# A single-core decode step: the last w_down rows in three transfers, ScalarE's softmax as a loop, one section at the end

## The chip, the cores and the metric

The kernel runs on one core of a Trainium2 chip. The metric is the device time of one execution in microseconds. The profile is one execution, taken by the hardware profiler; its span runs from the core's first instruction to its last.

In the profile PE is TensorE (matmul) and PEld its weight load, DVE is VectorE, ACT is ScalarE, POOL is GpSimd, and SP is the engine that issues nearly all loads. PEq, SPq and so on are the sequencers of these engines. DMA stands for the core's 16 DMA engines together.

## The reference, cut to what matters

One token (x has 1 x 1024 elements) passes through an attention block with a cache and a gated feed-forward block, in bf16.

```python
def _A_ref(x, k_cache, v_cache, wq, wo):        # 32 query heads, 4 key heads, 65536 keys of 128
    q = (x @ wq).reshape(B, Sq, Hq, Dh)          # k and v are repeated for the 8 heads of each group
    scores = einsum("bhqd,bhkd->bhqk", q, k) * Dh ** -0.5
    o = einsum("bhqk,bhkd->bhqd", softmax(scores), v)
    return o.reshape(B, Sq, Hq * Dh) @ wo

def _B_ref(x, w_gate, w_up, w_down):             # 1024 -> 3584 -> 1024
    return (gelu(x @ w_gate) * (x @ w_up)) @ w_down

h   = x + _A_ref(layernorm(x), k_cache, v_cache, wq, wo)
out = h + _B_ref(layernorm(h), w_gate, w_up, w_down)
```

Keys and values are 67 MB each, and the weights some 39 MB; all of it is read once.

## The kernel before

**Loads.** A ring of four slots of 4096 KB in on-chip memory (`slot`) takes every large load. SP issues them in one order: the two halves of wq, then for each step t of eight (four key heads, two halves of the keys) one load of V (8192 KB) into slots 0 and 1 and two of K (4096 KB each) into slots 2 and 3 for the next step, then wo, w_gate, w_up and w_down. SP waits on counters ahead of an issue: `s_qk` counts finished score chunks and frees K's slots, `s_step` counts five events of each step and frees V's slots. The five are the transpose of the maxima, their spread over all partitions, the first and the last of 64 matmuls that fill `acc`, and the last of four that make o (`o_ps`). What is issued is worked off in order by 16 DMA engines, each of which carries a sixteenth of every 128-partition transfer.

**A step of the loop.** VectorE transposes a chunk of K (`k_chunk`), TensorE multiplies it with the query (L450), VectorE transposes the scores back (`score`). After four chunks VectorE finds the maxima and spreads them with TensorE's help (`softmax`); ScalarE takes the exponentials in eight activations, one for each head of the group; TensorE multiplies them with V into `acc`; ScalarE copies `acc` to memory (`acc_copy`) and TensorE folds it into o. TensorE's side is a hardware loop of eight rounds (`pe_loop`); the loops of VectorE, ScalarE, GpSimd and SP are written out, instruction by instruction.

**Who orders the work.** The class `Flow` records the operations of the first part (everything up to the product of the gate and up branches) and writes them out engine by engine, with a counter of its own for each engine (`done_...`). A scheduler adds the switches between such hand-written sections and the rest: at a switch the engines wait for each other's counters.

**The end.** w_down has 28 rows for each partition. 16 come first (`wa`, the "first part"), then 8 (`wb`, the "eight rows"), then 3 and then 1 into a buffer of their own, `w_end`, by two transfers (L615) with semaphores of their own; the second is issued once VectorE is through with the first part (L610). TensorE keeps itself busy with four filler matmuls (`stay_busy`), multiplies the 16 rows as wide rows (`down_wide`, 32 matmuls), ScalarE copies the sums (L655), TensorE runs three more fillers and adds the copy to the result (`add_wide`, 8 matmuls), then multiplies the 8 rows (`down`, 64 matmuls of L624), the 3 rows (24 matmuls) and the last one (8 matmuls). The wide rows are one section, the eight rows another; the copy and the adding stand between them. VectorE and ScalarE cast the two halves of the result (L667, L668), and SP stores it.

Of the kernel before, what the change touches and what calls it, by code (L numbers as in the profile page):

```python
# [16 lines left out]
class Flow:  # L17


    def __init__(self, nc, tc):  # L20
        self.nc = nc
        self.tc = tc
        self.eng = dict(pe=nc.tensor, dve=nc.vector, act=nc.scalar, pool=nc.gpsimd, sp=nc.sync)
        self.sem = {e: tc.alloc_semaphore("done_" + e) for e in self.eng}
        self.ops = []
        self.writer = {}
        self.readers = {}
        self.rows = None, None
        self.landed = {}
# [36 lines left out]
    def loop(self, body):  # L66
        self.ops.append(dict(e="pe", call=body, loop=True, dma=False, inc=None))
# [14 lines left out]
    def issue(self):  # L82
        wanted = {j for o in self.ops for j in o.get("deps", ())}
        assert all(self.ops[j]["inc"] is None for j in wanted)
        count = dict.fromkeys(self.eng, 0)
        known = {e: {} for e in self.eng}
        token = {}
        for i, o in enumerate(self.ops):
            e = o["e"]
            if "loop" in o:  # L90
                o["call"]()
                continue
            if "given" in o:
                s, v = o["landed"]
                token[i] = (s.name, s, v, {})
                continue
            mine = known[e]
            waits = [(s.name, s, v, {}) for s, v in o["wait"]] + [token[j] for j in o["deps"]]
            for name, sem, v, seen in waits:
                if mine.get(name, 0) < v:  # L100
                    self.eng[e].wait_ge(sem, v)  # L101
                    mine[name] = v
                for n, x in seen.items():
                    mine[n] = max(mine.get(n, 0), x)
            ins = getattr(self.eng[e], o["call"])(**o["kw"])  # L105
            if o["inc"]:
                ins.then_inc(*o["inc"])
            elif o["dma"]:
                s, v = o["landed"]
                ins.then_inc(s, 16)  # L110
                token[i] = (s.name, s, v, dict(mine))
            elif i in wanted:
                count[e] += 1
                ins.then_inc(self.sem[e], 1)
                token[i] = ("done_" + e, self.sem[e], count[e], dict(mine))
# [3 lines left out]
def kernel(  # L119
# [14 lines left out]
    P = 128  # L134
# [77 lines left out]
    s_qk, s_step = [tc.alloc_semaphore("from_pe_%d" % i) for i in range(2)]  # L212
    STEPS = 5
# [9 lines left out]
    f.dma("act", x_in[:], A_x[0, 0].rearrange("(u v j) -> u v j", u=XU, j=DC), w=["x_in"], r=["ones_f"], sem=tc.alloc_semaphore("x_landed"))  # L223
# [17 lines left out]
    def v_load(t):  # L241
        g, h = divmod(t, NH)
        n0 = h * CPH * CH
        f.dma("sp", slot(0, 2).rearrange("p (n d) -> p n d", d=Dh), v_v[g][:, n0:n0 + CPH * CH, :], after=["R0", "R1"],
              wait=[(s_step, STEPS * t - 1)] if t else [], inc=(s_v, 16))
# [26 lines left out]
    op("pool", "tensor_copy", r=["ident_f"], w=["ident_bf"], out=ident_bf[:], in_=ident_f[:])  # L272
# [13 lines left out]
    select("o_of", o_of[:], ALU.is_ge, 0.0, 15, [[16, 8]], -1)  # L286
    HR = 30
# [44 lines left out]
    def rows_to_columns(banks, bkeys, key, order="p n -> p n", **sizes):  # L332

        w = [ps.shape[-1] for ps in banks]
        r = over(28672, [sum(w)])
        o = 0
        for ps, n, bk in zip(banks, w, bkeys):
            src = ps.rearrange(order, **sizes)
            op("dve", "transpose", r=[bk], w=[key], out=r[:, o:o + n].rearrange("p (e j) -> p e j", j=32) if sizes else r[:, o:o + n], in_=src)
            o += n  # L340
        return r[:, 0:o:32]
# [8 lines left out]
    op("dve", "tensor_copy", r=["q_r"], w=["q_bf"], out=q_bf[:].rearrange("p b m -> p (b m)"), in_=rows_to_columns(q_banks, ["B6", "B7"], "q_r"))  # L350
# [22 lines left out]
    op("pool", "memset", w=["qs"], ap=qs[:], constant=0.0)  # L373

# [14 lines left out]
    def score(t, c):  # L389
        n = t * CPH + c  # L390
        op("dve", "transpose", w=["sc%d" % c], wait=[(s_qk, n + 1)] + ([(s_step, STEPS * t - 2)] if t and c == 0 else []),
           out=sc[:, c].rearrange("p n h s -> p (n h s)"), in_=bank[n % 2][:])
        if c == CPH - 1:
            op("dve", "tensor_reduce", r=["sc%d" % x for x in range(CPH)], inc=(from_dve, 1), out=mx1[:],
               in_=sc[:].rearrange("p c n h s -> p h (c n) s"), axis=AX.XY, op=ALU.max)

    def o_copy(t):
        g, h = divmod(t, NH)
        op("dve", "tensor_copy", w=["o_raw%d" % t], wait=[(s_step, STEPS * t + 5)], out=o_raw[:, g, h, :], in_=o_ps)

    def softmax(t):
# [4 lines left out]
        op("dve", "tensor_scalar", w=["nb%d" % t], wait=[(s_step, STEPS * t + 2)], out=nb[:, g, h, :], in0=bc_ps, scalar1=-scale, scalar2=None, op0=ALU.mult)  # L406
        for r in range(rep):
            last = r == rep - 1
            op("act", "activation", r=["nb%d" % t] if r == 0 else [], w=[] if last else ["lp%d_%d" % (t, r)],
               inc=(from_act, 1) if last else None,  # L410
               out=pt[:].rearrange("p c n h s -> p (c n) h s")[:, :, r, :], in_=sc[:].rearrange("p c n h s -> p (c n) h s")[:, :, r, :],
               func=ACT.Exp, bias=nb[:, g, h, r:r + 1], scale=scale, accum_out=lp[:, g, h, r:r + 1])

    def acc_copy(t):
        op("act", "copy", wait=[(s_step, STEPS * t + 4)], inc=(from_act, 1), out=acc_sb[:], in_=acc[:])

    for t in range(NT2):
# [14 lines left out]
        if t + 1 < NT2:  # L432
            acc_copy(t)
# [4 lines left out]
    def pe_loop():  # L438
        v_sb = slot(0, 2).rearrange("p (c s n d) -> p c s n d", c=CPH, s=NS, d=Dh)
        with nc.Fori(0, NT2, engines=(mybir.EngineType.PE,), head_slot={mybir.EngineType.PE: 0}):  # L440
# [18 lines left out]
            for c in range(CPH):  # L459
                for n in range(NN):  # L460
# [6 lines left out]
                    if (c, n) == (CPH - 1, NN - 1):  # L467
                        m.then_inc(s_step, 1)
# [12 lines left out]
    op("dve", "tensor_tensor", r=keys("nb"), w=["mn"], out=mn[:], in0=nb[:, :, 0, :], in1=nb[:, :, 1, :], op=ALU.min)  # L481
    for h in range(NH):
        op("dve", "tensor_tensor", r=["mn"], w=["df%d" % h], out=df[:, :, h, :], in0=mn[:], in1=nb[:, :, h, :], op=ALU.subtract)
    op("act", "activation", r=["df0", "df1"], w=["fa"], out=fa[:], in_=df[:], func=ACT.Exp)
# [4 lines left out]
    acc_copy(NT2 - 1)  # L489
# [5 lines left out]
    for h in range(NH):  # L495
        op("dve", "tensor_tensor", r=["rl"], w=["wt%d" % h], out=wt[:, :, h, :], in0=fa[:, :, h, :], in1=rl[:], op=ALU.mult)
    o_copy(NT2 - 1)
    ow = sb("ow", [P, Hkv, NH, rep])
    op("dve", "tensor_tensor", r=["wt0", "wt1"] + keys("o_raw"), w=["ow"], out=ow[:], in0=o_raw[:], in1=wt[:], op=ALU.mult)
# [29 lines left out]
    f.dma("sp", wv[:, HC:Hq, :], wo_v[:, HC:Hq, :], w=["R3"], wait=done, sem=r_sem[2])  # L529
    for c in range(Hq):  # L530
# [26 lines left out]
    def ffn_in(wmat, key, s0, b0):  # L557
# [4 lines left out]
        f.dma("sp", wv, wmat.rearrange("(p c) n -> p c n", p=P), w=rk, sem=r_sem[s0], wait=[(s_step, STEPS * NT2 - 1)])  # L562
# [6 lines left out]
    op("dve", "tensor_tensor", r=["g_r"], w=["t1"], out=t1[:], in0=g_sb, in1=g_sb, op=ALU.mult)  # L569
    op("dve", "tensor_scalar", r=["t1"], w=["t1"], out=t1[:], in0=t1[:], scalar1=0.044715, scalar2=1.0, op0=ALU.mult, op1=ALU.add)  # L570
    op("dve", "tensor_tensor", r=["t1", "g_r"], w=["t1"], out=t1[:], in0=t1[:], in1=g_sb, op=ALU.mult)
# [3 lines left out]
    op("dve", "tensor_scalar", r=["g_r"], w=["hg"], out=hg[:], in0=g_sb, scalar1=0.5, scalar2=None, op0=ALU.mult)  # L575
# [24 lines left out]
    op("dve", "tensor_tensor", r=["u_r", "gl", "actz"], w=["actz"], out=actz[:, :, AZ], in0=u_r, in1=gl[:], op=ALU.mult)  # L600
# [3 lines left out]
    wb_src = B_w_down[P * FA:F, :].rearrange("(p e) n -> p e n", p=P)  # L604
# [9 lines left out]
    for i, (e1, e2) in enumerate(((FB - FZ, FB - 1), (FB - 1, FB))):  # L614
        d = nc.sync.dma_start(out=w_end[:, e1 - FB + FZ:e2 - FB + FZ, :], in_=wb_src[:, e1:e2, :])  # L615
        d.then_inc(end_sem[i], 16)
        tc.no_tile_sem_insts.add(d.ins.name)
        tc.keep_in_program_order(d)
        ends.append((d, e1, e2))

    def down(a_row, w_row, landed=None):
        for j in (0, 4, 1, 5, 2, 6, 3, 7):
# [3 lines left out]
            if landed is not None:  # L626
                tc.declare_no_dep(mm.ins, landed.ins, query=mybir.DependencyQuery.ANY, reason="TensorE waits for the load's own semaphore ahead of it")
# [8 lines left out]
    def down_wide(a_row, w_row, e, n):  # L636
        for h in range(DS):
            q = 2 * (e % 2) + h
            nc.tensor.matmul(e_ps[32 * q:32 * q + 32, :], lhsT=a_row[:, AZ:AZ + 32], rhs=w_row[:, h * NB:(h + 1) * NB],
                             start=(e < 2), stop=(e >= n - 2), tile_position=(0, 32 * q))  # L640

# [8 lines left out]
    with tc.tile_critical(no_gpsimd_drain=True):  # L650
        stay_busy(4)
        nc.tensor.wait_ge(sem, at)
        for e in range(n):
            down_wide(actz[:, a0 + e, :], w_rows[:, e, :], e, n)
    nc.scalar.copy(out=e_sb[:], in_=e_ps[:])  # L655
    stay_busy(3)
    add_wide()
    with tc.tile_critical(no_gpsimd_drain=True):
# [3 lines left out]
    for i, (d, e1, e2) in enumerate(ends):  # L662
        nc.tensor.wait_ge(end_sem[i], 16)
# [36 lines left out]
```

## Time and profile before

| | |
|---|---|
| Median of 3 runs | 409.56 us (409.26 to 409.87) |
| The profiled execution's own time | 409.4 us |
| Its span | 407.7 us |
| Read from memory | 173.02 MB, 424 GB/s over the span |
| Busy: PE, DVE, ACT, POOL | 57%, 49%, 10%, 4% |
| Share of the 16 DMA engines, loads of SP | 98.5% |
| Last load issued, landed | 395.25 us, 404.80 us |
| Mean granted TensorE clock | 0.807 |

The span lies 1.7 us below the execution's own time. Shares of busy time are averages over stages: the DMA engines work through all of them, the compute engines by turns. A line such as "404.84 0.35 PE bank L624 x8" in the chain of waits gives the start, the length, the engine, what was written and the source line; "issue" is time in which the profile shows nothing that was waited for. L105 is the line from which `Flow` writes everything it recorded, so groups of that line are told apart by what they write and read.

### The profile page before, as it was taken

What the parts mean: (1) busy time and instruction counts of PE and PEld (TensorE: products, weight loads), DVE (VectorE), ACT (ScalarE), POOL (GpSimd) and SP (SyncE); (2) the same over time, 40 slices, a digit from 0 to 9 for tenths busy, and PEclk for the clock granted to TensorE, in tenths of its full rate; (3) what the DMA queues carried; (4) which work ended last, traced back from release to release, by engine and by line L of the source; (5) the groups of instructions that cost most, each with busy time, mean ns of one, the idle gap of its engine ahead of it and who ended that gap; (6) DMA issues with size and microseconds to landing.
All of it is one profiled execution on the core that took longest, in us unless ns stands there. A gap on an engine that the chain in (4) does not pass through costs nothing. (4 is left out here: it accounts for less than half of the span.)

```text
span 407.7 us, 3720 instructions
## 1 busy us (share of the span) xinstructions
PE 232.5 (57%) x1558; PEld 102.8 (25%) x1558; DVE 201.2 (49%) x160; ACT 40.0 (10%) x142; POOL 16.7 (4%) x27
## 2 busy tenths in 40 slices
PE   0433745684476378726873685468456636635376
PEld 0211312232232133213321232233123213222322
DVE  2228850885089327834862696088508941020110
ACT  1000003000400210031003000300030022000000
POOL 4210000001000000010000001000000000030000
PEclk9999995698689866977895899569958977755569
DMA  8999999999999999999999999999999999999995
GB/s 360 412 450 423 440 434 412 460 418 432 434 460 418 412 444 469 424 405 418 489 424 395 434 424 453 412 466 412 412 457 457 424 405 421 464 444 440 391 418 217
DMA packets 4958, 173.10 MB, mean 425 GB/s; under 512 B 596, under 2 KB 600, under 8 KB 856
## 3 DMA queue, kind: packets, MB, share of 16 engines
q1 hardware_dynamic: 4904, 173.02, 98.5%
q8 instruction: 4, 0.07, 0.1%
q14 instruction: 2, 0.02, 0.0%
q10 hardware_dynamic: 48, 0.00, 0.0%
HBM read 173.02 MB, written 0.00 MB: 424 GB/s over the span
## 5 line engine op out<-in xcount | busy, mean ns | idle before, releaser
L105 DVE STREAM_TRANSPOSE ktb<-ring 128x4096 f32<-128x4096 f32 x32 | 141.2, 4419 | 73.4 <-DMA ring<-in_A_k_cache_dram 73.4
L450 PE MATMUL bank<-ktb,qs 128*128 128x512 bf16 x512 | 131.0, 415 | 52.0 <-PEq L436 52.0
L450 PEld LDWEIGHTS bank<-ktb,qs 128*128 128x128 bf16 x512 | 51.3, 103 | 128.5 <-issue 82.0
L462 PE MATMUL bank<-ring,pt 128*32 128x512 bf16 x512 | 45.3, 530 | 36.6 <-PEq L436 36.6
L105 ACT ACTIVATE pt<-sc,nb 128x256 bf16<-128x256 f32 x64 | 31.5, 493 | 255.6 <-DVE nb L105 255.6
L105 DVE STREAM_TRANSPOSE sc<-bank 128x512 f32<-128x512 f32 x32 | 22.3, 696 | 37.3 <-PE bank L450 37.3
L462 PEld LDWEIGHTS bank<-ring,pt 128*32 128x32 bf16 x512 | 19.0, 128 | 59.7 <-issue 56.4
L105 PE MATMUL bank<-ring,xz 128*32 128x512 bf16 (+1 forms) x192 | 18.2, 561 | 20.9 <-DMA ring<-in_B_w_gate_dram 8.9
L105 DVE STREAM_TRANSPOSE ktb<-bank 128x512 f32<-128x512 f32 (+1 forms) x6 | 4.0, 672 | 34.1 <-PE bank L105 33.8
L105 DVE TENSOR_REDUCE mx<-sc 128x8 f32<-128x2048 f32 x8 | 18.3, 2286 | 0.3
L454 PE MATMUL bank<-ident_f,mx 128*8 128x128 f32 x8 | 2.7, 333 | 25.8 <-PEq L436 25.8
L105 PEld LDWEIGHTS bank<-ring,xz 128*32 128x32 bf16 x192 | 7.2, 136 | 30.4 <-issue 19.1
L105 POOL COPY qs<-qsel 128x512 bf16<-128x512 bf16 x4 | 5.3, 1326 | 232.7 <-PE bank L450 218.6
L105 ACT ACTIVATION_READ_ACCUMULATOR pt<-sc,nb 128x1 f32 x64 | 11.9, 187 | 0.0
L471 PE MATMUL bank<-sel,acc_sb 128*128 128x8 f32 x64 | 8.2, 255 | 6.2 <-PEq L436 6.2
L471 PEld LDWEIGHTS bank<-sel,acc_sb 128*128 128x128 f32 x64 | 7.7, 191 | 10.0 <-issue 10.0
L105 ACT COPY acc_sb<-bank 128x512 f32<-128x512 f32 x8 | 4.7, 586 | 47.9 <-PE bank L462 47.9
L454 PEld LDWEIGHTS bank<-ident_f,mx 128*8 128x8 f32 x8 | 0.7, 83 | 29.5 <-issue 29.5
L105 PE MATMUL bank<-ring,ktb 128*32 128x512 bf16 x64 | 6.2, 554 | 2.8 <-DMA ring<-in_A_wo_dram 2.1
L456 PE MATMUL bank<-diag,ones_f 8*128 8x8 f32 x16 | 3.9, 312 | 5.7 <-PEq L436 5.7
L105 POOL MEMSET ktb<- 128x1024 bf16 (+2 forms) x3 | 3.5, 1165 | 76.3 <-PE bank L450 76.3
L105 DVE TENSOR_TENSOR h_col<-bank,x_col 128x8 f32<-128x8 f32 x1 | 0.2, 167 | 11.4 <-PE bank L105 11.4
(97 smaller groups left out, 64.9 us busy)
## 6 DMA issues: line engine op xcount, KB each, us to landing
ring<-in_A_k_cache_dram SPq DMA_DIRECT2D x16, 4096.0 KB, 24.8
ring<-in_A_wq_dram SPq DMA_DIRECT2D x2, 4096.0 KB, 16.6
ring<-in_A_wo_dram SPq DMA_DIRECT2D x2, 4096.0 KB, 25.1
ring<-in_B_w_gate_dram SPq DMA_DIRECT2D x1, 7168.0 KB, 27.2
ring<-in_B_w_up_dram SPq DMA_DIRECT2D x1, 7168.0 KB, 30.9
ring<-in_B_w_down_dram SPq DMA_DIRECT2D x1, 4096.0 KB, 21.0
ring<-in_B_w_down_dram SPq DMA_DIRECT2D x1, 2048.0 KB, 25.5
w_end<-in_B_w_down_dram SPq DMA_DIRECT2D x1, 768.0 KB, 25.7
```

The costliest lines, as they stand in the source:

```text
L105: ins = getattr(self.eng[e], o["call"])(**o["kw"])
L450: m = nc.tensor.matmul(bank[c][:], lhsT=qs[:, jt].rearrange("p s c -> p (s c)")[:, s * P:(s + 1) * P], rhs=mv[:, :, J, :, u], start=(s == ...
L454: nc.tensor.transpose(out=mxT_ps, in_=mx1[:], identity=ident_f[:]).then_inc(s_step, 1)
L456: nc.tensor.matmul(bc_ps, lhsT=ones_f[0:rep, :], rhs=diag[:], start=True, stop=True).then_inc(s_step, 1)
L462: m = nc.tensor.matmul(acc[32 * q:32 * q + 32, :], lhsT=pt[:, c, n, :, :].rearrange("p h s -> p (h s)"), rhs=v_sb[:, c, :, n, :], start=(c ...
L471: m = nc.tensor.matmul(o_ps, lhsT=acc_sb[:, u * Dh:(u + 1) * Dh], rhs=sel[:, u:SQ:NS], start=(u == 0), stop=(u == NS - 1))
```

## The change

- The last of the 28 rows, before one transfer of 128 partitions, is loaded by three: the 57 odd partitions from 1 to 113, the seven odd ones from 115 to 127, and the 64 even ones. All three count on one semaphore, and TensorE waits for 48 in place of 16.
- ScalarE's eight activations and the copy of `acc` become a hardware loop of eight rounds (`act_loop`); two semaphores, `act_go` and `s_acc`, hand it the start of a softmax and the end of `acc`. One small activation is added ahead of the loop.
- The last acc matmul now counts on `s_acc`, so `s_step` counts four events for each step. Waits that stood for the last acc matmul (the V load, the loads of w_gate) now stand for the last of the o matmuls. The wait ahead of `mn` is for the first acc matmul of the last step, and ScalarE's `fa` comes after the loop.
- TensorE's and ScalarE's work from the fillers to the eight rows is one section, with plain semaphores between the two engines.
- Smaller: the fill of `qs` and the copy `ident_bf` go from GpSimd to VectorE; two pairs of VectorE operations (`df`, `wt`) become one each; a wait list puts `done_` counters last; SP has no such counter; the load of x uses a semaphore that was there; the two transposes of `rows_to_columns` have keys of their own.

```diff
-    STEPS = 5
+    STEPS = 4
...
         f.dma("sp", slot(0, 2).rearrange("p (n d) -> p n d", d=Dh), v_v[g][:, n0:n0 + CPH * CH, :], after=["R0", "R1"],
-              wait=[(s_step, STEPS * t - 1)] if t else [], inc=(s_v, 16))
+              wait=[(s_step, STEPS * t)] if t else [], inc=(s_v, 16))
...
-        for r in range(rep):
-            last = r == rep - 1
-            op("act", "activation", r=["nb%d" % t] if r == 0 else [], w=[] if last else ["lp%d_%d" % (t, r)],
...
-    def acc_copy(t):
-        op("act", "copy", wait=[(s_step, STEPS * t + 4)], inc=(from_act, 1), out=acc_sb[:], in_=acc[:])
+    def act_loop():
+        with nc.scalar.Fori(0, NT2) as t:
+            nc.scalar.wait_ge(act_go, 1).then_inc(act_go, -1)
+            nb_t = nb[:].rearrange("p g h r -> p (g h) r")[:, bass.ds(t, 1), :].rearrange("p t r -> p (t r)")
+            lp_t = lp[:].rearrange("p g h r -> p (g h) r")[:, bass.ds(t, 1), :].rearrange("p t r -> p (t r)")
+            for r in range(rep):
+                m = nc.scalar.activation(out=pt[:].rearrange("p c n h s -> p (c n) h s")[:, :, r, :], in_=sc[:].rearrange("p c n h s -> p (c n) h s")[:, :, r, :],
+                                         func=ACT.Exp, bias=nb_t[:, r:r + 1], scale=scale, accum_out=lp_t[:, r:r + 1])
+            m.then_inc(from_act, 1)
+            nc.scalar.wait_ge(s_acc, 1).then_inc(s_acc, -1)
+            nc.scalar.copy(out=acc_sb[:], in_=acc[:]).then_inc(from_act, 1)
+
+    e_one = sb("e_one", [P, 1])
+    op("act", "activation", r=["ones_f"], w=["e_one"], out=e_one[:], in_=ones_f[:, 0:1], func=ACT.Exp)
+    f.loop(act_loop, "act")
...
                     if (c, n) == (CPH - 1, NN - 1):
-                        m.then_inc(s_step, 1)
+                        m.then_inc(s_acc, 1)
...
-    op("dve", "tensor_tensor", r=keys("nb"), w=["mn"], out=mn[:], in0=nb[:, :, 0, :], in1=nb[:, :, 1, :], op=ALU.min)
-    for h in range(NH):
-        op("dve", "tensor_tensor", r=["mn"], w=["df%d" % h], out=df[:, :, h, :], in0=mn[:], in1=nb[:, :, h, :], op=ALU.subtract)
+    op("dve", "tensor_tensor", w=["mn"], wait=[(s_step, STEPS * NT2 - 1)], out=mn[:], in0=nb[:, :, 0, :], in1=nb[:, :, 1, :], op=ALU.min)
+    op("dve", "tensor_tensor", r=["mn"], w=["df"], out=df[:], in0=mn[:].unsqueeze(2).to_broadcast([P, Hkv, NH, rep]), in1=nb[:], op=ALU.subtract)
...
-        f.dma("sp", wv, wmat.rearrange("(p c) n -> p c n", p=P), w=rk, sem=r_sem[s0], wait=[(s_step, STEPS * NT2 - 1)])
+        f.dma("sp", wv, wmat.rearrange("(p c) n -> p c n", p=P), w=rk, sem=r_sem[s0], wait=[(s_step, STEPS * NT2)])
...
-    for i, (e1, e2) in enumerate(((FB - FZ, FB - 1), (FB - 1, FB))):
-        d = nc.sync.dma_start(out=w_end[:, e1 - FB + FZ:e2 - FB + FZ, :], in_=wb_src[:, e1:e2, :])
-        d.then_inc(end_sem[i], 16)
...
+    odd = [57, 7]
+    for i, (e1, e2, rows) in enumerate(((FB - FZ, FB - 1, [slice(0, P)]),
+                                        (FB - 1, FB, [slice(1, 2 * odd[0], 2), slice(2 * odd[0] + 1, P, 2), slice(0, P, 2)]))):
+        loads = []
+        for p in rows:
+            d = nc.sync.dma_start(out=w_end[p, e1 - FB + FZ:e2 - FB + FZ, :], in_=wb_src[p, e1:e2, :])
+            d.then_inc(end_sem[i], 16)
...
         for e in range(n):
-            down_wide(actz[:, a0 + e, :], w_rows[:, e, :], e, n)
-    nc.scalar.copy(out=e_sb[:], in_=e_ps[:])
-    stay_busy(3)
-    add_wide()
-    with tc.tile_critical(no_gpsimd_drain=True):
+            mm = down_wide(actz[:, a0 + e, :], w_rows[:, e, :], e, n)
+        mm.then_inc(s_step, 1)
+        nc.scalar.wait_ge(s_step, STEPS * NT2 + 1)
+        nc.scalar.copy(out=e_sb[:], in_=e_ps[:]).then_inc(from_act, 1)
+        stay_busy(3)
+        nc.tensor.wait_ge(from_act, 1)
+        add_wide()
         nc.tensor.wait_ge(sem2, at2)
         for e in range(n2):
             down(actz[:, a2 + e, :], w_rows2[:, e, :])
     for i, (d, e1, e2) in enumerate(ends):
-        nc.tensor.wait_ge(end_sem[i], 16)
+        nc.tensor.wait_ge(end_sem[i], 16 * len(d))
```

## The prediction

> **What bounds the kernel now.** I read the profile's page first: the busy slices, then its DMA queues.
>
> ```profile
> DVE  2228850885089327834862696088508941020110
> DMA  8999999999999999999999999999999999999995
> ...
> q1 hardware_dynamic: 4904, 173.02, 98.5%
> q8 instruction: 4, 0.07, 0.1%
> q14 instruction: 2, 0.02, 0.0%
> ```
>
> No compute engine is full, but the 16 DMA engines are: 98.5% of the span goes to loads from q1. The instruction lines, six code fetches, look like nothing at 0.1%; they come back below. Next come the stretches of the end (last columns: DMA share, GB/s).
>
> ```profile
> 398.00:400.00 2.00, 2.00 (x28) 0.77 (x24) 0.00 (x0) 0.00 (x0) 0.00 (x0) 0.66 1.00 425
> ...
> 402.00:403.00 1.00, 0.17 (x14) 0.17 (x16) 0.00 (x0) 0.00 (x0) 0.00 (x0) 1.00 0.75 285
> 403.00:404.00 1.00, 0.91 (x64) 0.74 (x56) 0.00 (x0) 0.00 (x0) 0.00 (x0) 1.00 0.25 98
> 404.00:405.00 1.00, 0.68 (x32) 0.47 (x32) 0.00 (x0) 0.00 (x0) 0.00 (x0) 1.00 0.04 14
> ```
>
> The DMA engines stop one by one: for two microseconds a few still run while most are done. The chain that ended last and the timeline show what hangs on the last of them.
>
> ```profile
> 395.25 9.55 DMA w_end<-in_B_w_down_dram
> 404.80 0.04 issue
> 404.84 0.35 PE bank L624 x8
> 405.19 0.02 issue
> 405.21 0.26 ACT h L668
> ```
>
> After the landing at 404.80 come eight matmuls, two casts (405.17 and 405.21, both done by 405.47), the issue of the output at 405.54, and the closing barrier at 407.7.
>
> Who is late is in the trace's packet records. Each engine that carries a share of a transfer ends it with a 4-byte packet that counts up its semaphore, so 16 such packets per transfer say how far each engine lags behind the first (us, the last five):
>
> ```
> transfer whose first 4-byte packet starts at 31.50: 0.27 0.31 0.34 0.37 0.41
>                                              41.18: 0.27 0.31 0.34 0.37 1.93
>                                             108.99: 0.34 0.34 0.37 1.25 1.96
>                                             147.76: 0.34 0.37 1.03 1.27 1.98
>                                             368.30: 0.35 1.06 1.29 1.92 2.01
>                                             385.29: 1.01 1.23 1.50 1.86 1.96
> ```
>
> One more engine falls behind after each code fetch (16 KB at 33.1, 8 KB at 100.8 and 144.5, 16 KB at 351.7 and 376.8), and none ever catches up, because the queues never run dry: in the packet records no engine pauses for over 0.02 us between 2 and 402 us except at such a fetch. The fetch at 402.5 met an engine already done. So at the end eleven engines signal the last transfer at 402.92 to 403.21, five at 403.88, 404.12, 404.40, 404.72 and 404.80. Only three things can move the time: the last two engines, the 2.9 us after them, or a queue running dry.
>
> **The change part by part.** *Three transfers for the last row.* Before, it is 128 packets of 2 KB, eight per engine, each starting 0.080 us after the one before. Now 57, 7 and 64 partitions go separately. How 57 and 7 are spread is in no row. The rows that come nearest are three even splits: 128 partitions on 16 engines, 32 (the load of x) on 16 by two, and 4 (the output) on 4, where the semaphore shows one update at 406.00 and four at 406.68 to 406.73. An even split of 57 = 3 x 19 has 19 packets on each of 3 engines, of 7 one on each of 7, of 64 four on each of 16. Three engines then carry 24 packets, four carry 5, nine carry 4. Bounds: spread over all 16 nothing moves (0); all 57 on one engine, below. I take the split by 3, the same pattern as those three rows.
>
> [...]
>
> For a late engine among the nine this removes 4 x 0.080 = 0.32 us (three packets, 0.24, among the four): 404.80 becomes 404.48 (404.56). An early engine among the three gains 16 packets, 1.28: 402.92 to 403.21 becomes 404.20 to 404.49. Both groups end together, so the landing moves by 0.24 to 0.32. Packets to partitions that another engine is filling may slow each other; no row shows it, and I let it take up to the whole gain. Taken: **-0.3**. Which engines are late is not in the records; that the 1.28 added just fills the gap that the late ones leave is why I put them outside the three.
>
> *Two more DMA issues.* SP issues them after 395.25, and TensorE now enters its section only behind SP's next no-op, so they stand on its path. A lone issue takes 0.33; back-to-back ones took 0.42 and 0.52 at 1.94 and 2.41, but one at 376.80 took 1.37. I take 0.33 + 0.42 + 0.52 and 0.1 of gaps: SP is through at 396.6. The entry (two hops and a branch, 0.4) gives the first filler matmul at 397.1 instead of 395.88. Four fillers (1.79 before), the first part's 32 matmuls (397.67 to 400.39, 2.72), ScalarE's copy (0.59), the hops (0.3) and the eight adding matmuls (0.39) then end at 402.8. The 64 matmuls of the eight rows began at 402.83 although their data was signalled at 402.30; TensorE was going through section switches. Now no switch stands there, and they begin at 402.9: **0**, the delay of the issues paid by the merge. They issue for 0.86; the exit hop over SP that the merge adds has to end before the three-row landing (404.16). Margin 0.2.
>
> *ScalarE's loop.* Its built program shrinks from 166 to 67 instructions. The 8 KB fetch at 144.5, during ScalarE's third softmax, should go or move to the tail; that engine is 1.0 behind, not last: 0. Each softmax gains a wait and eight register instructions. An activation starts every 0.49 us; even eight instructions at TensorE's longest loop branch (0.21) in series give 1.7 us per step; as they can hide under the activation before, I take 0.2.
>
> *One step fewer on the counter.* The V load, and the gate weights after the last step, wait for the o matmuls instead of the last of the 64 that fill acc: by the last step, 343.54 becomes 345.31, +1.8. Behind the wait on SP stand the next two K loads, which wait longer for scores anyway. The shortest cover is at step 4: V issued at 189.70, first engine through with K at 196.25, first packet about 1.0 after an issue (0.81 to 1.83): 6.55 - 1.0 - 1.8 - 0.2 = 3.5 us left. So **0**; without this cover every lost microsecond would count eight times.
>
> *Small edits.* VectorE gets ident_bf and the fill of qs ahead of x, which lands at 9.26 (0). In the last step mn waits for the first acc matmul and fa comes behind the last acc copy, so lw and lsum end near 345 and the l matmul waits perhaps 0.2; two merged VectorE pairs give that back. The second half of wo lands at 353.88 and hides all of it (0). The sorted waits and split transpose keys add no work. The last activation at the start uses a table that is loaded there already.
>
> **Sum.** -0.3 + 0 + 0. The profiled execution took 409.4 (span 407.7, 1.7 around it) and would take 409.1; the median is 409.56, 0.16 above the profile, which gives 409.3. About 0.2%, 0.82 us, is what a measurement of this kernel can tell from no change, so this lies within it, at 0.3.
>
> **Rivals.**
> 1. *A late engine is among the three.* Its end goes to 404.80 + 1.28, about 410.8, slower. For it: two of sixteen are 1.9 behind and nothing in the records numbers them. Against: the room above fits. One that is only 1.0 to 1.2 behind would cost 0.3 to 0.6, and stay "same". Chance of slower 0.09.
> 2. *SP's issues take the place of the section switch.* If two cost 1.37 like the one at 376.80, SP is through 1.8 later; the 64 matmuls start at 404.7, the last eight end at 406.05 instead of 405.19: 410.4. It decides once the three issues pass about 1.6 us together. For: that one row. Against: it coincides with the code fetch at 376.8, and the issues at the start. Chance 0.05 (half of it over the bound).
> 3. *A queue runs dry.* If ScalarE's loop costs over 3.5 us more per step, the V load is late. The row against it is TensorE's own loop: eight rounds, and the fetches near it only at 33.1 and 351.7. At 5.5 us the eight steps, whose covers run from 3.5 to 4.8, lose 0.7 to 2.0 each, about 11 in all: 420, slower. Chance 0.02.
>
>    [...]
> 4. *The 57 go elsewhere.* Spread over 16: 409.6, same, 0.12. On one engine: 62 packets for 8, 54 x 0.080 = 4.3 on 403.2 gives 407.5 for 404.8: 412.2, slower, 0.03.
> 5. *More lateness goes.* If the fetches leave the last engines too, the landing falls to 403.2, and TensorE's chain (64, 24 and 8 matmuls from 402.83) ends 0.75 earlier: 408.8. Chance of over 0.82: 0.06.
>
> The forecast itself (gain of 0.1 to 0.4): 0.45; the rest of "same" is rival 4's first half, the small cases of 1 and 2 and lost gain. Together: faster 0.06, same 0.77, slower 0.17. The range 408.8 to 410.5 takes in rivals 2 and 5 and leaves out most of 1, 3 and the far end of 4.
>
> **What would show it.** Right: 24 packets on three engines, late ones signalling near 404.5, the 64 matmuls starting by 403.0, no fetch near 144, fillers starting near 397. Wrong: any engine idle before 402, V loads landing later than before, a fetch in every step of ScalarE's loop, or the last signal after 404.8.

## The result, and the profile after

The changed kernel took 410.38 us (median of 22 executions, 409.33 to 411.42) against 409.44 for the kernel before (22 executions, 409.17 to 410.11). The ratio is 1.0020, with a 95% interval of 1.0014 to 1.0027: slower by 0.8 to 0.9 us, small but clear of no change. The forecast was a gain of 0.3; its range held the time, its direction did not.

The spread is part of the result. The profiled execution, 409.35 (span 407.6), is one of the quickest of the changed kernel, so it shows what the change does when nothing goes against it. Two later profiles, of 409.89 and 410.69, show the rest and come further down.

First the DMA queues of the page (packets, MB, share).

```profile
q1 hardware_dynamic: 4914, 173.02, 98.6%
q8 instruction: 4, 0.07, 0.1%
...
q14 instruction: 1, 0.01, 0.0%
```

The queue stays as full as before, and one code fetch, ScalarE's at 144.5, is gone. Now the stretches of the end (TensorE's granted clock, DMA share and GB/s last) and the chain that ended last.

```profile
398.00:400.00 2.00, 2.00 (x24) 0.69 (x20) 0.00 (x0) 0.00 (x0) 0.00 (x0) 0.50 1.01 431
...
402.00:403.00 1.00, 1.00 (x44) 0.83 (x48) 0.00 (x0) 0.00 (x0) 0.00 (x0) 1.00 0.59 215
403.00:404.00 1.00, 0.57 (x44) 0.39 (x29) 0.00 (x0) 0.00 (x0) 0.00 (x0) 1.00 0.42 141
404.00:405.00 1.00, 0.56 (x32) 0.49 (x32) 0.00 (x0) 0.00 (x0) 0.00 (x0) 1.00 0.03 10
```

```profile
376.43 27.87 DMA w_end<-in_B_w_down_dram
404.30 0.14 issue
404.44 0.68 PE bank L631 x32
405.12 0.02 issue
405.14 0.26 ACT h L678
```

The releaser at the end is another transfer: no longer the last row, whose final signal came at 404.70 (404.80 before), but the three rows ahead of it, at 404.30. All 32 matmuls of the four end rows then run in one go and end at 405.12, 0.07 earlier than before. That is all the split brought in this execution.

SP's part and TensorE's, from the timeline of the same execution:

```profile
394.04 2.22 SPq L621 DMA_DIRECT2D w_end<-in_B_w_down_dram  x3
396.69 0.55 PEld L638 LDWEIGHTS bank<-qs 128*128 128x128 bf16 x4 [4.83 <-issue]
396.92 0.98 PE L638 MATMUL bank<-qs 128*128 128x512 bf16 x3 [4.62 <-SPq L658]
...
397.83 3.38 PE L646 MATMUL bank<-ring,ktb 128*32 128x512 bf16 x32
...
402.49 1.08 PE L631 MATMUL bank<-ring,ktb 128*32 128x128 bf16 x64
```

The three issues take 2.22 us, not 1.35, and TensorE's first filler (L638) waited for SP's no-op (L658). Only three of the four fillers left a matmul record; the four weight loads put the first filler at 396.69. Here SP began them early, at 394.04, and the 64 matmuls still started at 402.49.

### The profile page after: what moved, and what is told of

It reads as the page before. It is cut to its first block, busy times and chain, and to the rows that moved or that the text cites. A ratio compares the mean times of both kernels' runs of the same rounds, so it can differ in the third digit from the quotient of the medians.

```text
span 407.6 us, 3816 instructions
## 1 busy us (share of the span) xinstructions
PE 225.4 (55%) x1557; PEld 99.4 (24%) x1558; DVE 201.1 (49%) x160; ACT 40.2 (10%) x143; POOL 14.7 (4%) x25
## 5 line engine op out<-in xcount | busy, mean ns | idle before, releaser
L467 PE MATMUL bank<-ring,pt 128*32 128x512 bf16 x512 | 43.4, 513 | 38.0 <-PEq L441 38.0
L105 PE MATMUL bank<-ring,xz 128*32 128x512 bf16 (+1 forms) x192 | 16.0, 506 | 24.6 <-DMA ring<-in_B_w_gate_dram 9.9
L105 PEld LDWEIGHTS bank<-ring,xz 128*32 128x32 bf16 x192 | 6.3, 126 | 33.2 <-issue 15.9
L414 ACT ACTIVATION_READ_ACCUMULATOR pt<-sc,nb x64 | 12.0, 187 | 0.0
```

The source lines that it names most:

```text
L414: m = nc.scalar.activation(out=pt[:].rearrange("p c n h s -> p (c n) h s")[:, :, r, :], in_=sc[:].rearrange("p c n h s -> p (c n) h s")[:, ...
L467: m = nc.tensor.matmul(acc[32 * q:32 * q + 32, :], lhsT=pt[:, c, n, :, :].rearrange("p h s -> p (h s)"), rhs=v_sb[:, c, :, n, :], start=(c ...
```

## The experiments

Each run names the kernel it edits. "Start of the 64" is the first matmul of the eight rows before the end rows. Theories 1 to 3 are set out in the first expectation, theory 4 in that of the uneven row.

**The split undone.** The changed kernel with

```diff
-   (FB - 1, FB, [slice(1, 2 * odd[0], 2), slice(2 * odd[0] + 1, P, 2), slice(0, P, 2)])
+   (FB - 1, FB, [slice(0, P)])
```

> The changed kernel with the last row again in one transfer over all 128 partitions: 8 packets on every engine, one SP issue instead of three; loop, merged section and shorter counter stay. Theory 1 (an engine that is 1 to 2 us late through code fetches is among the three that carry 24 packets in some executions and not in others): median 409.4, within 0.2 of the kernel before, and executions as close together as those of the kernel before (within about 1 us). Theory 2 (the 1.3 us of the two more SP issues, in front of TensorE's section): also 409.4, or a little under, since the issues go. Theory 3 (the loss is in the rest: ScalarE's loop, the later V and gate waits, the merged section): 410.4, as the changed kernel, executions over 2 us apart.

Measured: 409.38 (409.24 to 409.91), ratio to the kernel before 0.9996 (0.9987 to 1.0005). Theory 3 is out: the loop, the later V and gate loads, the merged section and the small edits together cost nothing that shows. The loss comes with the three transfers.

**The split alone.** The kernel before, with only the three transfers and a wait for 48.

> The kernel before with only the last row in three transfers of 57, 7 and 64 partitions. Theory 1: the whole loss is there, 410.2 to 410.5, and executions spread over about 2 us (409.3 to 411.4). Theory 2: 409.4 to 411.0, more than the changed kernel, since the two issues are there and the section switches are not merged away. Theory 3: 409.4, narrow.

Measured: 409.81 (409.65 to 410.21), ratio 1.0006 (0.9997 to 1.0016), so 0.3 us that the measurement can't quite tell from no change, and narrow. None of the three expectations holds: it lies between theory 3's 409.4 and theory 1's 410.2, and below the changed kernel, where theory 2 put it above. There SP's issues do not stand ahead of TensorE's section (first filler at 394.86), and the chain of the profiled execution, 410.21, ends on a landing:

```profile
395.92 9.65 DMA w_end<-in_B_w_down_dram
405.58 0.04 issue
405.62 0.35 PE bank L629 x8
```

The last three signals, 405.19, 405.37 and 405.58, stand 0.56 behind all others, as the three shares of one engine would. TensorE's code fetch at 403.53 took 1.31 us in this kernel; in the changed one it comes at 401.49, before the shares differ. That the fetch hit a loaded engine is likely but not shown.

**Three transfers, evenly.** The changed kernel with `odd = [48, 16]`.

> The changed kernel with the last row in three transfers again, but of 48, 16 and 64 partitions: by the divisor of the partitions every engine has 3 + 1 + 4 = 8 packets, as in one transfer, while SP still issues three. Theory 1: 409.4 and narrow, as the kernel before. Theory 2 (the issues): 410.4, as the changed kernel. Theory 3: 410.4.

Measured: 409.70 (409.44 to 410.95), ratio 1.0007 (0.9998 to 1.0016). The last row has 48 signals, as 3 x 16, so in an even split no engine carries more than another, and yet three of the eleven executions pass 410.3. The profiled one, 410.58, had all landings by 404.83; the 64 matmuls started only at 404.34, after issues of 1.87 us. That is the wait that theory 2 expects; the median lies between the 409.4 of theory 1 and the 410.4 of theory 2.

**One engine overloaded.** The changed kernel with `odd = [59, 5]`.

> The changed kernel with 59, 5 and 64 partitions. 59 is prime, so one engine should carry 59 + 1 + 4 = 64 packets of 2 KB, 56 more than in one transfer, 4.5 us at 0.080 each. It is then always the last, and the time tells how late this one engine is in each execution. Theory 1: its landing is 407.5 if it is an early engine and up to 409.4 if it is one of the late ones, so the times lie between 412.1 and 414.0 and spread over 1 to 2 us. Theory 2 and theory 3 (a fixed loss of 0.9 that has nothing to do with which engine is late): 412.1 to 413.0 with executions within 0.5 us of each other.

Measured: 412.16 (412.03 to 412.32, 5 executions), ratio 1.0062 (1.0048 to 1.0075). The landing was at 407.54, the 407.5 of an early engine, and no execution was later by more than 0.3. In these five executions at least, this engine was never among the late ones, against theory 1.

**Issued early.** The changed kernel with the end loads' loop in

```diff
+   with tc.high_priority():
        for i, (e1, e2, rows) in enumerate(...):
```

which puts the three issues at 377.27 to 379.47, ahead of SP's no-op at 394.53.

> The changed kernel with one edit: the last row's three transfers of 57, 7 and 64 partitions are issued right behind the three-row transfer (near 377 to 380), ahead of SP's no-op that ends the first section, so that TensorE's section no longer stands behind them. Bytes, queue order and packets per engine stay. Theory 2 (the issues, 1.9 to 2.9 us for three in the profiles so far, start TensorE's chain of fillers, 32 matmuls, 8 and 64 late, and a lower granted clock stretches it): TensorE's section starts about 2 us earlier, the chain is covered again by the three-row landing at 404.2 to 404.4, and most of the 0.9 goes: 409.3 to 409.8. Theory 1 (late engines among the three with 24 packets): nothing changes, median 410.4, range 409.3 to 411.4. If both act, the remainder is what the split alone cost on the kernel before, 0.2 to 0.7, so 409.6 to 410.1.

Measured: 409.43, and the eleven executions lie between 409.37 and 409.45; ratio to the kernel before 0.9997 (0.9988 to 1.0006). The split, its bytes and its 24 packets on three engines are all there; the loss and the spread are gone. The timeline of the matmuls:

```profile
394.97 1.75 PE L639 MATMUL bank<-qs 128*128 128x512 bf16 x4 [2.11 <-SPq L659]
...
397.37 2.48 PE L647 MATMUL bank<-ring,ktb 128*32 128x512 bf16 x32 [0.65 <-DMA ring<-in_B_w_down_dram]
...
402.26 1.08 PE L632 MATMUL bank<-ring,ktb 128*32 128x128 bf16 x64 [1.06 <-DMA ring<-in_B_w_down_dram]
```

TensorE starts 2 us earlier and now waits for its data twice, 0.65 and 1.06 us: the chain is covered again. Theory 2 holds, theory 1 falls.

**Five issues.** The changed kernel with four transfers of 16 partitions and one of 64 for the last row.

> The changed kernel with the last row in five transfers of 16, 16, 16, 16 and 64 partitions: again 8 packets on every engine, but SP issues five times in front of TensorE's section instead of three. Theory 2: two more issues at 0.6 each start TensorE's chain 1.2 us later than with 48, 16 and 64, whose profiled execution took 410.58 and whose median was 409.70: 410.7 to 411.8. Theory 1: the balance is even, so 409.4 to 409.7 as with three even transfers.

Measured: 410.62 (410.18 to 411.78), ratio 1.0025 (1.0016 to 1.0035). The balance is even, the issues took 3.08 us, and the time rises with them. The median is just under theory 2's 410.7.

**Two more profiles of the changed kernel**, without an edit.

> The changed kernel once more, unedited, to see in a profile what its slower executions wait for. Theory 2: in an execution above 410 the last matmuls wait for TensorE's own chain (the 64 matmuls of the eight rows start after 403.2) and not for a landing. Theory 1: they wait for the last row's landing after 405, and the 64 matmuls started by 402.9.

> A second look at the changed kernel, unedited, with the same two expectations as the first: after 403.2 for the 64 matmuls (theory 2), or a last-row landing after 405 with the 64 matmuls by 402.9 (theory 1).

The first of these executions took 410.69. Its chain that ended last holds no transfer in its last 9 us:

```profile
397.42 0.02 SPq L658
397.44 0.30 issue
397.74 1.89 PE bank L638 x4
399.63 3.56 PE bank L646 x32
403.19 0.02 issue
403.22 0.59 ACT e_sb L665
...
404.44 0.74 PEld bank L631 x52
405.18 0.39 PEldq L658
405.57 0.02 SPq L658
...
405.77 0.68 PE bank L631 x32
```

It begins at SP's no-op and runs through TensorE's section to its exit over SP; the three rows (404.32) and the last row (404.65) had long landed. SP began its issues at 395.10 and needed 2.21 us. Its stretches (clock third from the end):

```profile
400.00:402.00 2.00, 2.00 (x24) 0.76 (x20) 0.00 (x0) 0.00 (x0) 0.00 (x0) 0.50 0.96 394
402.00:403.00 1.00, 1.00 (x12) 0.16 (x4) 0.00 (x0) 0.00 (x0) 0.00 (x0) 0.50 0.66 221
403.00:404.00 1.00, 1.00 (x9) 0.36 (x7) 0.00 (x0) 0.59 (x1) 0.00 (x0) 0.98 0.33 121
```

The granted clock stays at 0.50 until 403; with early issues it was 0.86 at 398 to 400 and 1.00 after:

```profile
398.00:400.00 2.00, 2.00 (x29) 0.68 (x22) 0.00 (x0) 0.09 (x1) 0.00 (x0) 0.86 0.98 417
400.00:402.00 2.00, 1.21 (x11) 0.52 (x9) 0.00 (x0) 0.49 (x1) 0.00 (x0) 1.00 0.96 391
```

So the 32 matmuls take 3.60 us here against 2.48 there. In the quick execution of the same kernel they took 3.38, but its fillers ran mostly at full clock: from the first filler to the end of the 32 it needed 4.52 us (396.69 to 401.21), the first look 5.42 (397.74 to 403.16). The second look, 409.89, is neither theory's case: its 64 matmuls started at 403.07, the landing of the three rows came half a microsecond late, at 404.84, and set the end. The whole queue was that late by then (the up weights landed at 388.09, in the other two profiles of this kernel at 387.57 and 387.62); why is open.

Profiled executions of the kernels whose end is set near TensorE's section, in the order of what SP issues ahead of it. The half-clock column is the stretch around the fillers in which the trace's record of the granted clock says 0.50:

```
issues ahead of the section    took   first filler   half clock         start of the 64   time     median
none (issued early)              -      394.97       395.15 to 398.57       402.26       409.40   409.43
128 partitions                  0.33    395.69       395.69 to 399.11       402.41       409.44   409.38
128 x 3, by columns             1.28    396.55       395.67 to 402.49       403.51       409.74   409.46
48, 16, 64                      1.87    397.46       396.39 to 403.21       404.34       410.58   409.70
57, 7, 64 (quick execution)     2.22    396.69       397.43 to 400.84       402.49       409.35   410.38
57, 7, 64 (second look)         2.21    397.27       398.15 to 401.56       403.07       409.89   410.38
57, 7, 64 (first look)          2.21    397.74       396.21 to 403.04       404.44       410.69   410.38
16 x 4, 64                      3.08    399.01       396.99 to 403.81       405.48       411.78   410.62
```

From 403.5 on the time is the start of the 64 plus 6.23 to 6.30 (409.74 - 403.51, 410.58 - 404.34, 410.69 - 404.44, 411.78 - 405.48); before that a landing sets it, and it is 409.4, or 409.9 in the second look.

Between the quick execution and the first look of the changed kernel the 64 start 1.95 us apart, after issues of the same length. SP began them 1.06 later (395.10 against 394.04); the half-clock column explains the other 0.9. Each stretch lasted 3.41 us or twice that. Where the first filler came ahead of it or with it, it lasted 3.41, and from the first filler to the 64 the changed kernel took 5.8 us; where the filler came 0.9 to 2.0 us after its start, it lasted 6.83, and that chain took 6.5 to 7.0. The other six profiles agree (two stretches with 59 partitions, filler 398.73 against 396.77; one in the five others, filler ahead). This was read from the profiles afterwards; no run set where the stretch begins.

**The uneven row first.** Early issues, `57, 7, 64` for the first of the four end rows, the last row in one transfer.

> The kernel with the early issues, and the uneven split moved from the last of the four end rows to the first of them: 57, 7 and 64 partitions for row 0, then rows 1 and 2 and then the last row in one even transfer each. Packets per engine over all four rows are as in the changed kernel, only their order differs. Theory 4 (the split did shorten the late engines, but the gain of 0.3 was never to be had behind it: the three-row landing at 404.35 plus 32 matmuls, 0.14 + 0.68, ends as late as before): now the three rows land at 404.0 on the late engines, the last row at 404.5, only 8 matmuls follow it, and the time is 409.1 to 409.2. If the late engines are among the three with 24 packets, or the split doesn't shorten the late ones, it is 409.4 or more.

Measured: 409.86 (409.71 to 410.06), ratio 1.0008 (0.9999 to 1.0017), not the gain of theory 4 but its other case, 409.4 or more. Even the transfer ahead of the end rows landed later, at 402.99 instead of 402.22, the three rows at 404.81 and the last at 405.44.

**Three rows unevenly.** Early issues, the three rows with `odd = [42, 22]`, and then with `[44, 20]`.

> Early issues, the last row in one even transfer, and the three rows (6 KB a partition) in transfers of 42, 22 and 64 partitions. By the divisors 42 goes to seven engines, 22 to eleven, 64 to sixteen: 36 packets of 2 KB on seven engines instead of 24 (+0.96 us), 18 on four (-0.48), 12 on five (-0.96). If none of the seven is a late one: their end goes from 403.2 to 404.2, the late ones from 404.8 to 404.3 or under, and the time is 408.7 to 409.0. If one that is 1.9 late is among the seven, its end goes to 405.8 and the time to 410.3 or so.

> As the run with 42, 22 and 64, but with 44, 20 and 64 partitions: eleven engines, ten, sixteen. Ten engines get 30 packets (+0.48 us), one 24, five 12 (-0.96). If the five late engines are the five with 12 packets, all end near 403.8 and TensorE's own chain sets the end: 408.4 to 408.8. If a 1.9-late engine is among the ten, its end goes to 405.3 and the time to 409.8. Together with the run on seven engines this tells whether the late engines have a fixed place.

Measured: 411.48 (411.44 to 411.64), ratio 1.0049 (1.0035 to 1.0063), and 411.65 (411.34 to 411.96), ratio 1.0053 (1.0040 to 1.0067). Both are beyond every case that was expected, so they tell nothing of where the late engines sit. That 42 partitions go to seven engines, 22 and 44 to eleven and 20 to ten was the author's estimate; no reading of these two runs shows it. The packet records say why the runs were slower (median ns of the packets that start in the stretch; 4 to 7 packets of 16 KB, 12 to 25 of 6 KB, 5 to 85 of 2 KB):

```
                              16 KB, 400-401   6 KB, 402-403   2 KB, 402-403
kernel before                      612              237             84
last row 57, 7, 64 (early)         611              247             84
last row 48, 16, 64                611              320            114
first row 57, 7, 64                886               -             115
three rows 42, 22, 64             1072              440            192
three rows 44, 20, 64             1108              516            200
```

The 16 KB packets belong to the eight rows, the transfer ahead: in the last three lines, with a transfer under way that is cut by partitions, the packets of this other one took up to 1.8 times as long (612 to 1108). The 6 KB packets of the last two rows are the cut transfer's own. With 57, 7 and 64 for the last row the effect is small in this stretch, 238 to 269 for 6 KB in the profiles of the changed kernel.

**Cut by columns.** The changed kernel with three transfers of all 128 partitions, 384, 384 and 256 columns.

> The changed kernel with the last row in three transfers cut by columns (384, 384 and 256 of its 1024) over all 128 partitions instead of by partitions. Every engine again has the same share of the same eight partitions as in one transfer, in three packets of 768, 768 and 512 bytes. If packets slow down wherever two engines fill neighbouring partitions (2 KB packets took up to 0.162 us and 6 KB packets up to 0.654 with 57, 7 and 64, against 0.093 and 0.246 at most in the kernel before), the 6 KB packets now stay at 0.23 to 0.25; if it is the number of transfers, they rise again to 0.27 or more. For the time, theory 2 (the issues ahead of TensorE's section) expects three issues of 0.33 to 0.6 each, so the chain starts between one issue (409.38) and 57, 7 and 64 (410.4): 409.4 to 410.0; theory 1 (late engines among the loaded ones) expects 409.4.

Measured: 409.46 (409.29 to 409.99), ratio 1.0002 (0.9993 to 1.0011). The 6 KB packets stay at 235 ns (249 at most) and SP's three issues take 0.33, 0.43 and 0.42. In these runs it is thus the cut by partitions that goes with slower 6 KB packets (320 ns with 48, 16 and 64, 440 and 516 with the three rows cut), not the number of transfers. (The 0.654 that was quoted as the largest with 57, 7 and 64 is no proof of it: one packet of the run with a single transfer shows 0.655 as well. The medians carry the reading.) Why packets slow down under such a cut no run here shows.

## Why the prediction was wrong

**The failed step: "Two more DMA issues ... 0".** It put the issues on TensorE's path rightly, and sized two terms too low, so that "the delay of the issues paid by the merge" did not hold. The three issues were to take 1.35 us with gaps; they took 2.2, because those of 57 and 7 partitions took 0.85 and 0.75 each. The rows taken, 0.33, 0.42 and 0.52, were of other shapes; three transfers of all 128 partitions cost nearly what those rows say, 1.28 in all. And from first filler to the 64 matmuls the step allowed 5.8 us (397.1 to 402.9; its terms add up to 402.9, not 402.8), from the kernel before's 2.72 us for the 32 matmuls. Measured were 5.8 in the quick execution and the second look, but 6.7 in the first look, 6.9 with 48, 16 and 64 and 7.0 with the columns, where the half-clock stretch was twice as long. In the first look the filler came at 397.74 instead of 397.1, and 6.7 us instead of 5.8 followed: together 1.5, which put the 64 matmuls at 404.44 instead of 402.9, against a margin named as 0.2. When SP comes earlier, as at 394.04, or the clock returns sooner, the loss shrinks to nothing; that is the difference between the quick execution and the first look, and the likely source of the spread. SP's start went with the clock too: it began the issues at 394.04, 394.63 and 395.10 where full clock had come back at 390.60, 391.32 and 392.80.

**Rival 2 is what happened**, in its mechanism: SP's issues took the place of the section switch. That its price, 410.4, meets the median, 410.38, is in part luck. It had SP through 1.8 us later than forecast (398.4) and the chain as forecast; in the first look SP was through 0.7 later, at 397.31, and the clock added 0.9. Its point of decision, 1.6 us for three issues, also took the clock as given: by columns 1.28 were enough for the 64 to start at 403.51 and for 409.74, in the execution that had the long stretch. It got 0.05 on the argument that its one long issue, 1.37, coincided with a code fetch; nothing fetched near 394 to 397, and the issue of 57 partitions took 0.85 all the same.

**The -0.3 of the split** was right for the last row and lost in front of it. The even splits hold in the semaphore's signals: 28 for 57, 7 and 64, as 3 + 7 + 16 and two at the issues; 24 for 59, 5 and 64, as 1 + 5 + 16 and two. In the changed kernel's three profiles and with early issues the last signal of the last row came 0.30 to 0.40 us after that of the three rows, where one even transfer needs 0.64 (404.16 to 404.80): the 0.24 to 0.32 that was forecast. But the last signal of the three rows came 2.09 to 2.15 after that of the eight rows, against 1.86 in the kernel before (402.30 to 404.16). The 6 KB packets that start from 402.4 on (from 402.9 in the second look, whose queue was late), those of the late engines, took 263 to 280 ns in the median in these four profiles, against 236 in the kernel before, and each engine has eight of them. So slower packets ate the gain, as the prediction allowed for when it let them "take up to the whole gain"; the last landing came at 404.65 to 404.70 in three of the profiles, 0.1 before 404.80. Nor was the whole to be had: the landing of the three rows, 404.16 before, plus 0.14 and 0.68 gives 404.98 against 405.19, so 0.2 was the most. The prediction listed what can move the time and left this wait out.

**Rival 1** (a late engine among the three) did not come: eleven executions within 0.08 us with early issues. The 59 partitions on one engine (64 packets) cost about what rival 4 gave for 62, 412.2.

**ScalarE's loop and the waits** cost nothing that shows, as forecast. This is the loop's activation in the changed kernel (busy us and mean ns behind the bar), 493 ns before:

```profile
L414 ACT ACTIVATE pt<-sc,nb 128x256 bf16<-128x256 f32 x64 | 31.5, 494 | 258.0 <-ACTq L410 258.0
```

The seven V loads that wait were issued 0.3 to 3.3 us later and the gate weights 3.2 (346.74), or 2.0 in the first look, where 1.8 was assumed. That term was too low, but the cover held: in the quick execution each V load landed 0.1 us earlier than before, and the queue never ran dry. The early issues with the split, 409.43, and the single transfer, 409.38, only match the kernel before; no version here beats it.

## What to carry to other kernels

Price an issue by a row of its own shape (0.85 us for 57 partitions here, 0.33 for 128), and ask which engine's section stands behind it: an issue that needs nothing can go out before the no-op that opens the section, and there it cost nothing here (409.43 against 409.44). The chain that was to be covered with 0.2 us to spare, with 2.72 us for its 32 matmuls, was not covered where they took 3.60 at a granted clock of 0.50, so size such a chain at the lowest clock that the profile shows nearby, for as long as it was seen to last. And before shortening the last landing, work out where the landing ahead of it would put the end.

## What the runs showed that was not expected

- Near 395, SP needed 0.85 us to issue 57 partitions, 0.75 for 59 or 7, 1.17 for 5, 0.52 to 0.61 for 64, 48 or 16 and 0.33 to 0.43 for 128. Of the signals of the 57 and the 7, one each comes with the issue, at 395.27 and 396.12, 6 to 7 us before the data.
- The 16 KB packets of a transfer over all 128 partitions took 612 ns in the median before, and 886, 1072 and 1108 ns while the first row (57, 7, 64) or the three rows (42, 22, 64 and 44, 20, 64) were loaded in a cut by partitions.
- TensorE's half-clock stretch around the fillers ends between 398.6 and 401.6 in nine profiles and between 402.5 and 403.8 in five, and lasts 3.41 or 6.83 us. In the kernel before and in the quick execution of the changed kernel the granted clock changes, over the whole span, only after whole multiples of 3.41 us (3.41 to 20.48), and from another starting point in each: the half-clock stretch around the fillers begins at 395.95 in the one and at 397.43 in the other. What sets that point no run here shows.
